# Loading x already transposed and running the 3x3 taps as 32x32 tiles, in a ConvNeXt V2 block

## The chip, the cores and the metric

The kernel runs on one NeuronCore of a Trainium2 chip. The core has a matrix engine (TensorE, PE in the profile; PEld is its loading of weights), three engines for elementwise work (VectorE is DVE, ScalarE is ACT, GpSimd is POOL) and SyncE (SP), which here only issues DMAs. Each engine runs its own instruction stream in order, and semaphores tie the streams together. The metric is device time in microseconds (us) of one execution; lower is better. The kernel before took 1479.03 us, the median of three runs (1475.51 to 1484.01).

## The reference

```
def reference(x, dw, w1, w2, grn_gamma, grn_beta):     # x: (1, 512, 512, 96), bf16
    xp = jnp.pad(x, ((0,0),(1,1),(1,1),(0,0)))
    out = 0
    for i in range(3):
        for j in range(3):
            out = out + xp[:, i:i+H, j:j+W, :] * dw[i, j]          # depthwise 3x3
    h = _layernorm(out, axis=-1)                                  # over the 96 channels
    h = gelu(einsum('bhwc,ce->bhwe', h, w1))                      # 96 -> 384, tanh form
    gx = sqrt((h * h).sum(axis=(1, 2)) + 1e-6)                    # per channel, over the whole image
    nx = gx / (gx.mean(axis=-1) + 1e-6)
    h = grn_gamma * (h * nx) + grn_beta + h
    return x + einsum('bhwe,ec->bhwc', h, w2)                     # 384 -> 96
```

The sum over all pixels in `gx` divides the work in two: nothing of the second product can start before every pixel has gone through the first.

## The kernel before

The image is cut into 128 blocks of 4 rows (2048 pixels). The first phase goes over the blocks in slots, one block a slot for each kind of work, and the kinds are staggered: in slot s the kernel loads x for block s+4, turns block s+3, convolves block s, and runs the first product and the GELU of a block about ten back. A table (`put`, `get`) says what each slot does. Every engine's instructions stay in the order in which the program is written (`InOrder`), so a waiting instruction holds up all that follows it on its engine.

The steps of a block:

- `load_x` (line 216): SP loads the block to `xin`, 128 partitions of 18 neighbouring pixels (16 and one at each side), 3456 bytes on each. Four buffers.
- `turn_x` (line 442): two DVE transposes of 32x32 blocks bring channels onto partitions, into one of five buffers `xT`. Channels 0 to 63 are turned as pairs, so two neighbouring channels lie side by side; `x_rows` (line 450) picks every second column for them.
- `conv_taps` (line 463): 72 matmuls with 64x32 tiles of the matrix engine (64 rows hold two groups of 32 partitions, 32 columns are channels), in three bursts of 24, from `Wq`, a weight tensor built at the start out of `Wd`. The two row halves of one moment write different PSUM banks. The result stands in `Y3`, PSUM banks 4 to 6, or in other banks in a few early slots (`spare`). `burst(0)` ends with a drain of the matrix engine in most slots.
- `evac` (line 496): one ACT instruction copies the three banks to `y_bf`.
- `stage_sq` (POOL, `ysq`), `stage_stats` (24 tiny matmuls that sum `y_bf` and `ysq` over channels), `stage_moments` (DVE), `stage_rstd` and `stage_newton` (POOL, a chain of small operations), `stage_turn` (DVE, `rt`), `stage_rows` (SP, to `r_dram`), `stage_bcast` (SP, four DMAs `rbc` that repeat a row over partitions): these make the layer norm's factor, for a batch of four blocks at a time.
- `stage_norm` (POOL, `yn`), `stage_write` (SP, four DMAs to `yn_dram`), `stage_read` (SP, `ynT`): the normalized block goes through DRAM to come back with 96 channels on partitions.
- `mlp_units` (line 699): the first product in units of one or two PSUM banks, each followed by an ACT instruction that applies GELU into `g`. A quarter of a block is either channel-major (cm: 384 output channels on partitions; DVE's `bn_stats` then gives the sums of squares) or pixel-major (px: the sums of squares come from 12 further matmuls, `gram_next`). `cm_quads` (line 100) says how many of a block's four quarters are cm. Blocks with q % 10 in 0, 3, 7 (`WHOLE`) are kept in DRAM (`g_dram`) with all four quarters cm.

The order written out for one slot with a conv and a first product (lines 886 to 923) is: `conv(0)`, unit(0,2), unit(2,1), squares, `conv(1)`, `turn_x(s+3)`, unit(3,1), unit(4,2), gram, ..., unit(7,1), turn, `conv(2)`, `evac`, gram, unit(8,2), unit(10,1), stats, unit(11,1). On SP the order of a slot is load_x, read, write, bcast, rows, one third of a g store (lines 828 to 838). On POOL it is newton, norm, sq, rstd (lines 839 to 846).

After the last slot the factor `nx` is computed and folded into `W2s`. The second phase then takes the blocks in a fixed order: it recomputes `g` from the normalized blocks, or loads it, or has it still in SBUF; it multiplies by `W2s`, adds x and stores. The change touches nothing that the second phase does, but for the order of columns within a quarter (`quad`, `quad_out`).

Of the kernel before, what the change touches and what calls it, by code (L numbers as in the profile page):

```python
# [9 lines left out]
ACTF = mybir.ActivationFunctionType  # L10
AX = mybir.AxisListType

GR = 4
# [6 lines left out]
WHOLE = (0, 3, 7)  # L20
# [36 lines left out]
def kernel(  # L57
# [11 lines left out]
    f32 = mybir.dt.float32  # L69
    i32 = mybir.dt.int32  # L70
    bf16 = x.dtype
    assert bf16 == mybir.dt.bfloat16

    B, H, W, C = x.shape
# [3 lines left out]
    NI = C // 32  # L78
    NCH = E // 128
    NG = W // 128  # L80
    NBLK = H // GR
    BATCHES = batches_of(NBLK)

    QW = GR * 128
    NQ = GR * W // QW
# [8 lines left out]
    def is_held(q):  # L94
        return q in HELD

    def is_whole(q):
        return q < TAIL0 and q % 10 in WHOLE

    def cm_quads(q):  # L100
        if is_whole(q) or is_held(q):
            return NQ
        if q > HELD[0]:
            return 1
        return 2 if q >= NBLK - 16 or (q - 1) % 10 in WHOLE else 3
# [4 lines left out]
    def chans(i):  # L110
        return slice(i, 64, 2) if i < 2 else slice(64, 96)

    PXP = GR * W // 128
    MB = W // PXP

    def quad(flat_ap, t):
        return flat_ap.rearrange("p r (t g m) -> p t g r m", t=NQ, m=MB)[:, t]

    def quad_out(flat_ap):
        return flat_ap.rearrange("p (g r m) -> p g r m", r=GR, m=MB)  # L120
# [10 lines left out]
    consts = ctx.enter_context(tc.tile_pool(name="consts", bufs=1))  # L131
# [9 lines left out]
    Wq = consts.tile([128, NI, 3, GR, 32], bf16, name="Wq")  # L141
# [12 lines left out]
    parts = consts.tile([128, NCH, NACC + 1], f32, name="parts")  # L154
# [24 lines left out]
    gpool = ctx.enter_context(tc.tile_pool(name="g", bufs=5))  # L179
# [3 lines left out]
    SL = PXP + 2  # L183
    with ExitStack() as p1:
        pe, dve, act, pool, sp = (InOrder(tc, e) for e in (nc.tensor, nc.vector, nc.scalar, nc.gpsimd, nc.sync))
# [3 lines left out]
        def banks(n):  # L189
            if n == 2:  # L190
                return PS[:, 0:2, :]
            ones[0] += 1
            return PS[:, 2 + ones[0] % 2:3 + ones[0] % 2, :]
# [14 lines left out]
        Y3 = PS[:, 4:7, :]  # L208
        pc = p1.enter_context(ExitStack())
        xinpool = pc.enter_context(tc.tile_pool(name="xin", side="right", bufs=4))  # L210
        xins = {}

        def shift(h, j):
            return 1 if (h, j) == (0, GR - 1) else -1 if (h, j) == (1, 0) else 0

        def load_x(b):
            t = xinpool.tile([128, SL, C], bf16, name="xin")
            off = x.offset + b * GR * W * C
            rows = lambda p0, p1, s0, s1: (
                t[p0:p1, s0:s1, :].rearrange("p g c -> p (g c)"),  # L220
                bass.AP(x.tensor, off + (p0 * PXP - 1 + s0) * C, [[PXP * C, p1 - p0], [1, (s1 - s0) * C]]))
            if b == 0:
                pool.memset(t[0:1, 0, :], 0.0)
                parts = [(16, 128, 0, SL), (0, 16, 1, SL), (1, 16, 0, 1)]
            elif b == NBLK - 1:
                pool.memset(t[96:128, SL - 1, :], 0.0)
                parts = [(0, 112, 0, SL), (112, 128, 0, SL - 1), (112, 127, SL - 1, SL)]
            else:
                parts = [(0, 128, 0, SL)]
            for part in parts:  # L230
                o, i_ = rows(*part)
                sp.dma_start(out=o, in_=i_)
            xins[b] = t

        Wd = gpool.tile([128, NQ, NCH, QW], bf16, name="g")[:].rearrange("p t j w -> p (t j w)")[
            :, :NI * 9 * 32].rearrange("p (i k c) -> p i k c", i=NI, k=9)
        zrow = consts.tile([128, W], bf16, name="zrow")
# [4 lines left out]
        for b in range(min(2, NBLK)):  # L242
            load_x(b)
        act.activation(out=warm[:], in_=warm[:], func=ACTF.Gelu_apprx_tanh)
        act.activation(out=Wq[:].rearrange("p i d j c -> p (i d j c)").rearrange("p (a w) -> p a w", a=3),
                       in_=zrow[:, None, :NI * GR * 32].to_broadcast([128, 3, NI * GR * 32]), func=ACTF.Identity)
# [8 lines left out]
        xtpool = pc.enter_context(tc.tile_pool(name="xt", side="right", bufs=1))  # L255
# [6 lines left out]
        NXT = 5  # L262
        xt_ring = []
        xt_all = xtpool.tile([128, NXT, NI, SL * MB], bf16, name="xT")
        for i in range(NXT):
            xt_ring.append(xt_all[:, i])
        assert NXT * NI * SL * MB >= NQ * NCH * QW
        g_over = xt_all[:].rearrange("p x i s -> p (x i s)")[:, :NQ * NCH * QW].rearrange(
# [123 lines left out]
        for i in range(NI):  # L392
            dve.tensor_copy(out=dwx[:, i], in_=dw9[:, None, chans(i)].to_broadcast([9, GR, 32]))
            pe.matmul(Ud[:, i, :], lhsT=dwx[:, i].rearrange("p q c -> p (q c)"), rhs=ident_b[:9, :9],
                      start=True, stop=True)
# [3 lines left out]
        n = 0  # L399
        for h in range(2):  # L400
            for j in range(GR):
                for q in (2 * h, 2 * h + 1):
                    a = q + GR * shift(h, j) - j + 1
                    if 0 <= a < 3:
                        n += 1
                        o, i_ = Wq[32 * q:32 * q + 32, :, :, j, :], Wd[32 * q:32 * q + 32, :, 3 * a:3 * a + 3, :]
                        if n % 2:
                            act.activation(out=o, in_=i_, func=ACTF.Identity)
                        elif n % 4:
                            dve.tensor_copy(out=o, in_=i_)  # L410
                        else:
                            pool.tensor_copy(out=o, in_=i_)

# [28 lines left out]
        def turn_x(b):  # L442
            xin = xins.pop(b)
            t = xt_ring[b % NXT]
            pairs = t[:, 0:2, :].rearrange("p i s -> p (i s)").bitcast(f32)
            dve.transpose(out=pairs.rearrange("p (g m) -> p g m", m=MB),
                          in_=xin[:, :, 0:64].bitcast(f32))
            dve.transpose(out=t[:, 2, :].rearrange("p (g m) -> p g m", m=MB), in_=xin[:, :, 64:96])

        def x_rows(b, p0, p1, i, c0, n):  # L450
            t = xt_ring[b % NXT]
            if i == 2:
                return t[p0:p1, 2, c0:c0 + n]
            return t[p0:p1, 0:2, :].rearrange("p i s -> p (i s)").rearrange(
                "p (s e) -> p s e", e=2)[:, c0:c0 + n, i]

# [6 lines left out]
        def conv_taps(b, spare):  # L463
            if spare:
                Ua, Ub = banks(2), banks(1)
                Y = [Ua[:, 0, :], Ua[:, 1, :], Ub[:, 0, :]]
            else:
                Y = [Y3[:, i, :] for i in range(NI)]
            mms = []
            for n in range(3):  # L470
                mms.append([(h, j, (n + h) % NI, dx) for dx in (0, -1, 1) for j in range(GR) for h in range(2)])
            flat = [m for ms in mms for m in ms]
            first = {}
            last = {}
            for n, (h, j, i, dx) in enumerate(flat):
                first.setdefault((i, j), n)
                last[i, j] = n

            def burst(n, fence=True):
                k = sum(len(ms) for ms in mms[:n])  # L480
                for h, j, i, dx in mms[n]:
                    src = b + shift(h, j)
                    o0, o1 = max(0, -dx), W - max(0, dx)
                    pe.matmul(
                        Y[i][32 * j:32 * j + 32, o0:o1],
                        lhsT=Wq[64 * h:64 * h + 64, i, dx + 1, j, :],
                        rhs=x_rows(src, 64 * h, 64 * h + 64, i, MB * (1 + dx) + o0, o1 - o0)
                        if 0 <= src < NBLK else zrow[64 * h:64 * h + 64, o0:o1],
                        start=first[i, j] == k,
                        stop=last[i, j] == k,  # L490
                    )
                    k += 1
                if n < 2 and fence:
                    pe.drain()

            def evac():
                y = ypool.tile([128, NI, W], bf16, name="y_bf")
                if spare:
                    act.activation(out=y[:, 0:2, :], in_=Ua, func=ACTF.Identity)
                    act.activation(out=y[:, 2, :], in_=Ub[:, 0, :], func=ACTF.Identity)  # L500
                else:
                    act.activation(out=y[:], in_=Y3, func=ACTF.Identity)
                ybf[b] = y

            return [lambda fence=True, n=n: burst(n, fence) for n in range(3)], evac
# [288 lines left out]
        for k, (b0, n) in enumerate(BATCHES):  # L794
# [16 lines left out]
            for b in range(b0, b0 + n):  # L811
# [4 lines left out]
                m = s + (3 if ramp else 4)  # L816
# [4 lines left out]

        busy(FILL[1])
        turn_x(0)
        turn_x(1)
        turn_x(2)
        for s in range(last_slot + 1):
# [34 lines left out]
            elif not mlp:  # L861
                if s + 3 < NBLK:
                    turn_x(s + 3)
# [21 lines left out]
            else:  # L885
                b = mlp[0]
# [9 lines left out]
                if s + 3 < NBLK:  # L896
                    turn_x(s + 3)
# [71 lines left out]
        r = gi[:].bitcast(f32)  # L969
        for it in range(3):  # L970
# [5 lines left out]
            r = rn_[:]  # L976
# [75 lines left out]
```

## Time and profile before

| what | value |
|---|---|
| median of three runs | 1479.03 us (1475.51 to 1484.01) |
| span of the profiled execution | 1480.8 us |
| mean granted TensorE clock | 0.994 |
| first phase, about | 0 to 960 us |
| second phase, about | 960 to 1480 us |
| blocks convolved per slot time, 200 to 490 us | one every 7.03 us |
| from 1100 to 1300 us: DMA share, POOL busy | 1.02, 193.79 of 200 us |

The page's second part is read first: it cuts the span into 40 slices of 37 us.

```profile
PE   8888999999999999999999997789999999999998
...
GB/s 180 179 205 255 241 253 280 228 271 260 260 248 264 258 264 255 276 253 254 263 258 266 263 216 195 195 225 409 366 359 402 417 416 413 419 410 417 411 412 282
```

Up to slice 25 is the first phase, from slice 27 on the second, where the DMA engines move some 410 GB/s. A group's line gives the number of instructions, their busy time together and the mean of one; what follows the bar is the time for which the engine stood idle just before them and what ended it. Busy times overlap: neighbouring instructions of one engine run into each other.

### The profile page before, as it was taken

To read this page: it belongs to the slowest core of one execution; us is meant where nothing else is said; L and a number is where in the kernel's file an instruction comes from. 1 tells how busy PE (TensorE), PEld (TensorE's weight loads), DVE (VectorE), ACT (ScalarE), POOL (GpSimd) and SP (SyncE) were. 2 spreads that over 40 slices of the span, in tenths; PEclk is the share of its full clock that TensorE was granted. 3 is DMA by queue.
4 is the path that set the end of the run, shared out by engine and by line. 5 is a ranking of instruction groups with operands and counts; after the bars stand their busy time and mean duration, and the time that the engine had idled before them with its cause. 6 is when DMAs were issued, how large, how long until landed. Compare 5 with 4: busy or idle time off the path is not lost.

```text
span 1480.8 us, 54225 instructions
## 1 busy us (share of the span) xinstructions
PE 1391.3 (94%) x23125; PEld 810.4 (55%) x23125; DVE 1182.0 (80%) x2135; ACT 1414.4 (96%) x1595; POOL 1300.3 (88%) x922
## 2 busy tenths in 40 slices
PE   8888999999999999999999997789999999999998
PEld 3434444444444444444444445467777777776776
DVE  7849989999999999999999987965555555555555
ACT  7888989999999999999999999999999999999997
POOL 3459889998998999998999987569999999999997
PEclk9999999999999999999999999999999999999999
DMA  5568788788888888888888866669999999999997
GB/s 180 179 205 255 241 253 280 228 271 260 260 248 264 258 264 255 276 253 254 263 258 266 263 216 195 195 225 409 366 359 402 417 416 413 419 410 417 411 412 282
DMA packets 167768, 433.08 MB, mean 292 GB/s; under 512 B 31558, under 2 KB 81318, under 8 KB 163046
## 3 DMA queue, kind: packets, MB, share of 16 engines
q1 hardware_dynamic: 151284, 326.04, 66.3%
q0 software_dynamic: 14880, 103.43, 17.6%
q8 instruction: 181, 2.97, 0.8%
q14 instruction: 61, 0.50, 0.1%
q10 hardware_dynamic: 1362, 0.15, 0.1%
HBM read 273.30 MB, written 156.22 MB: 290 GB/s over the span
## 4 chain that ended last, share of the span: by engine, by line
PE 30%; ACT 24%; DMA 19%; POOL 13%; DVE 6%; issue 4%; SPq 4%; POOLq 0%; ACTq 0%; DVEq 0%
PE PS L35 30%; ACT g L35 16%; DMA out_dram<-o_sb 9%; POOL yn L35 6%; ACT y_bf L35 5%; POOL ysq L35 5%; SPq L35 4%; DMA yn_dram<-yn 3%; DVE bst L35 3%; DMA xin<-in_x_dram 2%; DMA rbc<-r_dram 2%; DMA ynT<-yn_dram 1%; DMA g_dram<-g 1%; DVE o_sb L35 1%; ACT xT L35 1%
## 5 line engine op out<-in xcount | busy, mean ns | idle before, releaser
L35 ACT ACTIVATE g<-PS 128x512 bf16<-128x512 f32 (+2 forms) x1062 | 727.7, 864 | 16.5 <-PE PS L35 15.6
L35 DVE BATCH_NORM_STATS2 bst<-g 128x6 f32<-128x512 bf16 x1110 | 671.3, 672 | 35.4 <-ACT g L35 34.5
L35 PE MATMUL PS<-ynT,w1p 128*128 128x512 bf16 x2181 | 609.6, 381 | 23.6 <-ACT g L35 5.4
L35 ACT ACTIVATE gr<-PS 128x1536 bf16<-128x1536 f32 x360 | 498.5, 1459 | 18.8 <-PE PS L35 13.8
L35 POOL TENSOR_TENSOR yn<-y_bf,rbc 128x1536 bf16<-128x1536 bf16 x126 | 391.3, 3108 | 77.3 <-ACT rbc L35 21.9
L35 DVE TENSOR_TENSOR o_sb<-PS,xb 128x384 bf16<-128x384 f32 x512 | 277.3, 556 | 227.0 <-PE PS L35 190.1
L324 POOL TENSOR_TENSOR xb<-xr,B2c 128x1536 f32<-128x1536 bf16 x118 | 368.1, 3133 | 4.3 <-DVE o_sb L35 2.0
L35 PE MATMUL PS<-xT,Wq 64*32 64x511 bf16 (+1 forms) x9198 | 340.5, 389 | 26.2 <-ACT y_bf L35 8.1
L35 POOL TENSOR_TENSOR ysq<-y_bf 128x1536 bf16<-128x1536 bf16 x114 | 313.6, 2752 | 12.8 <-ACT y_bf L35 12.8
L35 PEld LDWEIGHTS <-w1p 128*128 128x128 bf16 x2181 | 171.6, 98 | 222.0 <-issue 133.4
L35 PEld LDWEIGHTS <-gr 128*128 128x128 bf16 x4296 | 212.1, 98 | 68.9 <-issue 12.0
L35 PE MATMUL PS<-W2s,gr 128*128 128x96 bf16 x4224 | 223.5, 206 | 8.2 <-DVE o_sb L35 8.0
L35 PEld LDWEIGHTS <-Wq 64*32 64x32 bf16 x9216 | 111.9, 90 | 193.3 <-issue 145.9
L35 ACT ACTIVATE y_bf<-PS 128x1536 bf16<-128x1536 f32 (+2 forms) x135 | 199.4, 1482 | 17.4 <-PE PS L35 13.3
L35 DVE STREAM_TRANSPOSE xT<-xin 128x576 f32<-128x576 f32 (+1 forms) x256 | 181.4, 748 | 8.1 <-DMA xin<-in_x_dram 8.1
L35 PEld LDWEIGHTS <-g 128*128 128x128 bf16 x1704 | 104.9, 98 | 86.3 <-issue 54.3
L35 PE MATMUL PS<-w1p,ynT 128*128 128x256 bf16 (+2 forms) x822 | 125.8, 273 | 8.0 <-ACT xT L35 3.2
L35 PE MATMUL PS<-g 128*128 128x128 bf16 x1464 | 122.6, 220 | 2.9 <-DVE PS L35 2.6
L35 PEld LDWEIGHTS <-gl 128*128 128x128 bf16 x1680 | 82.8, 98 | 26.8 <-issue 5.0
L35 PE MATMUL PS<-W2s,gl 128*128 128x96 bf16 x1680 | 89.5, 206 | 3.4 <-DVE o_sb L35 3.2
L35 PEld LDWEIGHTS <-ynT 128*128 128x128 bf16 x822 | 64.1, 97 | 31.5 <-issue 13.7
L279 POOL DMA_DIRECT2D xr<-in_x_dram x115 | 63.7, 555 | 14.2 <-POOL xb L324 14.2
(105 smaller groups left out, 576.5 us busy)
## 6 DMA issues: line engine op xcount, KB each, us to landing
xin<-in_x_dram SPq DMA_DIRECT2D x126, 432.0 KB
g_dram<-g SPq DMA_DIRECT2D x105, 512.0 KB
gl<-g_dram POOLq DMA_DIRECT2D x35, 1536.0 KB, 11.3
yn_dram<-yn SPq DMA_DIRECT2D x512, 96.0 KB
ynT<-yn_dram SPq DMA_DIRECT2D x128, 384.0 KB
out_dram<-o_sb SPq DMA_DIRECT2D x127, 384.0 KB
xr<-in_x_dram POOLq DMA_DIRECT2D x123, 384.0 KB, 6.9
ynT<-yn_dram SPq DMA_DIRECT2D x85, 512.0 KB
```

Source lines behind the costliest of these rows:

```text
L35: r = f(*a, **k)
L279: pq.dma_start(out=xr[:], in_=x[0, r0:r0 + GR].rearrange("r w c -> (r w) c").rearrange("(p g) c -> p g c", g=PXP))
L324: pq.tensor_tensor(out=xb[:], in0=grp[q]["xr"][:], in1=bias[:, None, :].to_broadcast([128, PXP, C]), op=ALU.add)
```

## The change

x is no longer loaded and then turned. One DMA per block reads the block's 512 runs of four pixels (4 x 96 values, 768 bytes) and writes them transposed: the 384 values of a run lie on 128 partitions in three groups k, and the runs lie along the free axis. `xT` is one ring of six blocks. `turn_x`, `x_rows`, `xin` and `Wq` are gone, and the matrix engine reads `Wd` itself.

A value's place now follows from its pixel's phase a (0 to 3 within the run) and channel group i (0 to 2): (k, r) = divmod(3a + i, 4), where r is the quarter of the partitions. A tap in x changes the phase, or at the edge of a run also the column by one; a tap in y shifts the columns by a row of 128. A tap for one phase and channel group is a matmul with a 32x32 tile, from partition quarter r to output quarter a. A block takes 108 such matmuls in three bursts of 36; where the six-block ring wraps (two blocks of six) and at the image's edges a tap in y is cut into two.

The output rows of a block come out ordered by phase, so `evac` reads PSUM with a step of four values and writes `y_bf` in the order that the rest expects, and `quad` and `quad_out` become runs of 128 columns. At last, blocks that follow a whole block have three cm quarters instead of two (34 blocks).

```
-        return 2 if q >= NBLK - 16 or (q - 1) % 10 in WHOLE else 3
+        return 2 if q >= NBLK - 16 else 3
...
-        return slice(i, 64, 2) if i < 2 else slice(64, 96)
+        return slice(32 * i, 32 * i + 32)
...
-        return flat_ap.rearrange("p r (t g m) -> p t g r m", t=NQ, m=MB)[:, t]
+        return flat_ap[:, :, t * 128:(t + 1) * 128]
...
+        NXT = 6
+        xt_all = xtpool.tile([128, NI, NXT * GR, W4], bf16, name="xT")
         def load_x(b):
-            t = xinpool.tile([128, SL, C], bf16, name="xin")
...
+            s0 = b % NXT * GR
+            sp.dma_start_transpose(
+                out=xt_all[:, :, s0:s0 + GR, :].rearrange("p k r w -> p k (r w)"),
+                in_=bass.AP(x.tensor, x.offset + b * GR * W * C, [[4 * C, GR * W4], [1, 4 * C]]))
...
-        def turn_x(b):
-            xin = xins.pop(b)
-            t = xt_ring[b % NXT]
-            pairs = t[:, 0:2, :].rearrange("p i s -> p (i s)").bitcast(f32)
-            dve.transpose(out=pairs.rearrange("p (g m) -> p g m", m=MB),
-                          in_=xin[:, :, 0:64].bitcast(f32))
-            dve.transpose(out=t[:, 2, :].rearrange("p (g m) -> p g m", m=MB), in_=xin[:, :, 64:96])
...
+            src = [(0, 0), (-1, 1), (1, 2)]
+            def rows_of(dy):
+                lo, hi = max(0, -dy), GR - max(0, dy)
+                out = [(lo, hi, b, lo + dy)]
+                if dy and 0 <= b + dy < NBLK:
+                    edge = 0 if dy < 0 else GR - 1
+                    out.append((edge, edge + 1, b + dy, GR - 1 - edge))
+                if len(out) == 2 and abs(out[1][2] % NXT - b % NXT) == 1:
+                    start = b % NXT * GR + dy
+                    return [(0, GR, start)]
+                return [(o0, o1, q % NXT * GR + r0) for o0, o1, q, r0 in out]
             def burst(n, fence=True):
+                dx = src[n][0]
+                for dy in (0, -1, 1):
+                    segs = rows_of(dy)
+                    for o0, o1, r0 in segs:
+                        for L in range(4 * NI):
+                            a, i = divmod(L, NI)
+                            a2 = a + dx
+                            w0, w1_ = (1, W4) if a2 < 0 else (0, W4 - 1) if a2 > 3 else (0, W4)
+                            v0 = w0 - 1 if a2 < 0 else w0 + 1 if a2 > 3 else w0
+                            k, r = divmod(a2 % 4 * NI + i, 4)
+                            pe.matmul(
+                                Y[i][32 * a:32 * a + 32, :].rearrange("p (r w) -> p r w", r=GR)[:, o0:o1, w0:w1_],
+                                lhsT=Wd[32 * r:32 * r + 32, i, 3 * (dy + 1) + dx + 1, :],
+                                rhs=xt_all[32 * r:32 * r + 32, k, r0:r0 + o1 - o0, v0:v0 + w1_ - w0],
...
+            def px_order(ps):
+                return ps.rearrange("p i (q e) -> p i e q", e=NQ)
+            def flat_order(y):
+                return y.rearrange("p i (e q) -> p i e q", e=NQ)
...
-                    act.activation(out=y[:], in_=Y3, func=ACTF.Identity)
+                    act.activation(out=flat_order(y[:]), in_=px_order(Y3), func=ACTF.Identity)
```

The calls of `turn_x` in the slots are gone with it. `load_x(s + 4)` stands where it stood on SP; it now overwrites the place of block s-2, whose last reader is the conv of block s-1, where it used to wait for a free `xin`.

## Prediction

> **What bounds the kernel now.** I read the totals first, then one long steady stretch by engines, then one slot in order of time, then the chain of waits and the DMA queues.
>
> ```profile
> PE 1391.3 (94%) x23125; PEld 810.4 (55%) x23125; DVE 1182.0 (80%) x2135; ACT 1414.4 (96%) x1595; POOL 1300.3 (88%) x922
> ...
> L35 DVE STREAM_TRANSPOSE xT<-xin 128x576 f32<-128x576 f32 (+1 forms) x256 | 181.4, 748 | 8.1 <-DMA xin<-in_x_dram 8.1
> ```
> ```profile
> 204.00:484.00 280.00, 269.00 (x4855) 131.47 (x4852) 278.16 (x477) 280.00 (x399) 258.72 (x188) 1.00 0.83 260
> ```
>
> The second line is the table by stretches (us, then busy time of PE, PEld, DVE, ACT, POOL, clock, DMA share): for 280 us ACT is never idle and DVE idles for 1.8 us. The 181.4 us of DVE transposes are the work to be removed, but an engine beside a full ACT gives nothing back. One slot shows what ACT's fullness consists of:
>
> ```profile
> 507.12 1.61 ACT L35 ACTIVATE y_bf<-PS 128x1536 bf16<-128x1536 f32 x1
> 508.46 5.97 ACT L35 ACTIVATE g<-PS 128x1024 bf16<-128x1024 f32 x9
> 508.79 0.88 PE L35 MATMUL PS<-xT,Wq 64*32 64x512 bf16 x24 [0.15 <-ACT y_bf L35]
> 509.77 0.82 PE L35 MATMUL PS<-ynT,w1p 128*128 128x512 bf16 x3
> ...
> 514.19 1.58 ACT L35 ACTIVATE y_bf<-PS 128x1536 bf16<-128x1536 f32 x1
> ```
>
> Slot: 514.19 - 507.12 = 7.07 us, one y_bf and nine GELUs. In the trace's starts an ACT instruction behind another takes 477 ns for 512 columns, 904 for 1024, 1331 for 1536; a slot's 6, 3 and 1 of them make 2.86 + 2.71 + 1.33 = 6.91 us. The remaining 0.12 to 0.15 us lie at one place: conv(0) may start only when y_bf has left Y3 (508.73), it takes until 509.7 with its drain, and the first GELU of the next block waits behind it. So conv(0), alone among the three bursts, stands on the path.
>
> The other thing on the path is the layer norm's loop:
>
> ```profile
> 491.35 2.75 POOL ysq L35
> ...
> 494.15 1.53 PE PS L35 x31
> ...
> 502.91 2.93 DMA g_dram<-g
> ...
> 506.11 3.11 POOL yn L35
> ```
>
> This is the chain of waits: start, length, what. POOL's yn at 506.11 stood still until a DMA had landed (the rbc just before it), and at 494.15 PE's sums waited for POOL's ysq. Between ysq's end and the matmuls that read it the trace has 5.4 us at 240 us, 3.1 at 293 and 0.1 at 494: every batch of four slots loses 5.3 / 9 = 0.59 us against ACT, and from 494 us on this loop holds ACT up. It runs: yn, ysq, rstd, newton, yn, ysq, yn on POOL (19.2 us), four yn_dram DMAs (2.6), four rbc DMAs (2.7), landing (3.5): 28.0 us against 4 slots of 7.03.
>
> ```profile
> q1 hardware_dynamic: 79947, 154.38, 82.2%
> ```
>
> That is SP's queue from 200 to 800 us: each DMA engine is busy for 0.83 x 7.03 = 5.83 us of a slot.
>
> **The change, part by part**, against the profiled execution of 1480.8 us, which lies 1.8 over the median.
>
> Removed: 256 DVE transposes (-181.4 us) and, with them, a turn in the slot's middle; added: 34 cm quarters, 34 x 3 bn_stats at 671.3 / 1110 = 605 ns, +62 us of DVE. DVE falls to about 1063 us and stays under ACT: 0 on the path. ACT covers it; without it the net 119 us would show. PE loses 34 x 12 matmuls of gram at 56 ns (-23 us), late in the slot, where PE already has 0.2 us of waiting for y_bf to give: 0, at best -20. The build of Wq goes; the first conv starts at 8.08 us, when the warm-up matmuls end: 0. In the ramp two yn wait 0.2 us behind a turn; I take -2 us, bounds 0 and -14 (all ACT idle time from 100 to 200 us and near 893 us, were the loop's stalls to go).
>
> Conv: 9216 matmuls become 15336. In a burst the trace starts eight tiles 3 to 7 ns apart, the next eight 216 ns after the first; twelve tiles make 4 x 6.5 = 26 ns more per burst. For conv(0) in some 105 slots: +3 us. Where the ring wraps (42 blocks) twelve more pairs follow, between 12 x 3 = 40 ns and, by the tiny sum matmuls, 12 x 25 = 300; at 0.1 us: +4. The other two bursts use PE's 0.2 us. Lower bound 0; upper bound, if only eight tiles overlap as now: 36 / 8 x 216 = 0.97 us for 0.65, +0.32 in 105 slots = +34. I take +7, since twelve differs from eight by less than from none.
>
> A rule speaks against this. Before, the tiles that run together write one bank per row half; now a bank is written by four row tiles at once, on different partition quarters. TensorEngine Tiling (Array Packing), Restrictions and Gotchas, says that different row tiles cannot use one PSUM bank at a time. By it a bank's four tiles would follow each other, three in parallel: 36 / 3 x 216 = 2.6 us a burst, and a slot would grow by almost 6 us. No row here shows two row tiles on one bank.
>
> evac reads PSUM with a step of four. No row reads PSUM so. The nearest is the small copy to Wq in pieces, 435 ns for 288 columns where the slope of the plain ones gives 163 + 0.84 x 288 = 405: bounds 0 and +7%, 0.1 us x 128 = +13. I take 0.
>
> The load: SP's issue was 430 ns (median). Bounds 300 ns, the quick rows of rbc, and 2.5 us, the four issues of yn_dram. I take 0.6; in the loop SP has 0.7 us to spare before the yn writes, so it hides; at 2.5 us some 1.4 stick out in 25 batches, +35. The load also has a new wait, for conv(s-1). Behind it on SP stand ynT, the yn writes and rbc; POOL waits for rbc, PE for ynT two slots on. At 277.39 and 284.65 us the load went out 3 us before that conv ended, but the yn writes then waited for POOL anyway; in the slot with rbc it was 0.7 us (266.14 against 266.85). That eats slack once: +2.
>
> The transfer itself: 8 packets of 3456 bytes per engine, 135 ns each (median), were 1.08 us. The new one reads 256-byte pieces, 96 per engine. Packets of 64 bytes take 11 ns and of 1024 bytes 46, so 18 for 256: 1.73 us, +0.65 per load. Bounds: the old rate per byte, 0.96 us (-0.12); and pieces of 32 bytes (16 rows of two bytes on a partition), 768 x 10 = 7.7 us (+6.6). I take 256-byte pieces, the nearer kind to what is read. The load stands in the rings before rbc, so the loop grows by about 0.6 us: 1.2 lost per batch instead of 0.59, the slack of 5.4 us at 240 us is gone after 4.5 batches, and 18 batches lose 1.2 where 14 lost 0.59: 22 - 8 = +14.
>
> DMA: Bandwidth & Descriptors, Latency and other measured facts, gives a transposing DMA 261 GB/s where rows are not contiguous. By it a load would be 1.5 us, and the +14 would shrink to about +8.
>
> Sum: 1480.8 - 2 + 7 + 2 + 14 = 1502 in the profiled execution, **1500** against the median.
>
> **Rivals.**
> Faster: the load costs an engine no more than before (-0.12 us), each block arrives three slots early instead of one, DVE answers the turn at once, and the loop's stalls (about 14 us of ACT idle time) go: 1479 - 14 = 1465. For it: DVE waited 8.1 us for xin, and rt came 4 us after newton. Against: ACT's floor of 6.91 us a slot stands. It decides as soon as a load takes under 1.3 us of each engine.
> No change: every term within 7 us of nothing: 1479.
> DMA becomes the bound: from 7.03 - 5.83 + 1.38 = 2.6 us per load on (1.38 is the old one's mean). At 4 us a slot lasts 8.45, and 118 of them give +168: about 1647; at the far bound, 7.7 us, 2083. For it: a DMA share of 0.83 leaves little. Against: fewer bytes than before.
> SP becomes the bound: its issues fill 0.72 of a slot; at 2.5 us per load it is full, 1535 as worked out above.
> That the tiles do not overlap gives 1479 + 34 = 1513, within the forecast's range.
>
> **How the numbers follow.** Forecast 0.42, faster 0.24, no change 0.14, DMA-bound 0.13, SP-bound 0.07. A measurement of this kernel tells 0.5% (7.4 us) from no change. Faster by more: 0.24 + 0.02 of the forecast's low side = 0.26; same: 0.14; slower: 0.60. The likeliest case alone spans 1487 to 1530 (the terms at 0 and the conv at its upper bound). The range goes down to 1460, the faster case with 5 us to spare, and up to 1580, a load of 3.4 us; that leaves out some 0.08 above and 0.07 below.
>
> **What would show it.** Right: DVE near 1063 us and idle in every slot, ACT above 98% from 204 to 484 us, slots of 7.05 to 7.15, conv bursts of 24 ns more, POOL's yn waiting for rbc in more batches and before 400 us, a DMA share of 0.87 to 0.92. Wrong: a DMA share at 1.0 with PE and ACT idle in the first phase; bursts over 1 us; issues of xT on SP over 1.5 us; y_bf above 1.45 us where it stands alone; or a first phase shorter than 950 us, which would say that the loop and not ACT set it.

## The result, and the profile after

The changed kernel takes 1542.33 us, the median of four runs (1538.77 to 1547.03), where the kernel before takes 1480.74 beside it: a ratio of 1.041, with a 95% interval from 1.0377 to 1.0444. It is slower by 62 us (56 to 66); 1500 was forecast. The profiled execution spans 1540.4 us, 59.6 more than that of before, and the explanation is made against these 59.6.

First, where in the span they lie. The trace gives every start of `y_bf`, one for a block (two for the seven blocks in other banks). The 28th start marks the end of the ramp, the last one the end of the convolutions:

| us | ramp, to the 28th y_bf | steady, 28th to last (106 blocks) | rest | span |
|---|---|---|---|---|
| before | 132.2 | 751.5 | 597.1 | 1480.8 |
| changed | 141.4 | 802.6 | 596.4 | 1540.4 |

So 9 us go in the ramp, 51 in the steady stretch, and nothing after it. The engines' totals and the table by stretches of the changed kernel, in the columns shown for the kernel before:

```profile
PE 1402.1 (91%) x28735; PEld 852.5 (55%) x28735; DVE 1088.7 (71%) x1982; ACT 1416.7 (92%) x1588; POOL 1296.1 (84%) x917
```
```profile
204.00:484.00 280.00, 253.63 (x6185) 134.75 (x6165) 237.18 (x407) 263.69 (x374) 244.47 (x186) 0.98 1.04 237
```

DVE is relieved of its transposes, ACT has as much to do as before (1416.7 against 1414.4). But in the 280 us in which ACT was never idle it now stands still for 16.3, no engine is full, and the DMA share has gone from 0.83 to 1.04 while fewer bytes move (237 against 260 GB/s). That share suggests that the DMA engines are the bound; the experiments will show that SP's issues are the larger part. One slot, in the timeline (start, length, engine, instructions, idle time before them):

```profile
499.59 1.58 ACT L35 ACTIVATE y_bf<-PS 128x1536 bf16<-128x1536 f32 x1
501.22 0.86 PE L35 MATMUL PS<-xT,Wd 32*32 32x512 bf16 x36 [0.16 <-ACT y_bf L35]
506.57 1.63 ACT L35 ACTIVATE y_bf<-PS 128x1536 bf16<-128x1536 f32 x1
```

An undisturbed slot still lasts 506.57 - 499.59 = 6.98 us, and a burst of 36 takes no longer than a burst of 24 did (0.86 against 0.88). The loss is in some slots only, about one in four. Such a one, with SP's queue and POOL in order of time:

```profile
439.92 2.10 SPq L35 DMA_DIRECT2D yn_dram<-yn  x2
442.06 2.08 SPq L35 DMA_DIRECT2D rbc<-r_dram  x4
444.24 1.85 SPq L35 DMA_TRANSPOSE xT<-in_x_dram  x1
446.20 0.51 SPq L35 DMA_DIRECT2D ynT<-yn_dram  x1
446.77 2.50 SPq L35 DMA_DIRECT2D yn_dram<-yn  x4
447.94 3.10 POOL L35 TENSOR_TENSOR yn<-y_bf,rbc 128x1536 bf16<-128x1536 bf16 x1 [3.55 <-DMA rbc<-r_dram]
...
450.00 2.50 SPq L35 DMA_TRANSPOSE xT<-in_x_dram  x1
...
461.25 2.75 POOL L35 TENSOR_TENSOR ysq<-y_bf 128x1536 bf16<-128x1536 bf16 x1
464.06 0.45 PE L35 MATMUL PS<-rowsel,ysq 128*128 128x4 bf16 x12 [3.19 <-POOL ysq L35]
464.79 0.60 ACT L35 ACTIVATE g<-PS 128x512 bf16<-128x512 f32 x1 [1.86 <-PE PS L35]
```

Read it downwards. From 439.92 to 449 SP hardly rests: one issue follows the other within 0.1 us. The four `rbc` come out at 442.06, when SP has got to them; POOL has waited 3.55 us when they have landed, its `ysq` ends 3 us late two slots on, PE's sums wait 3.19 us for it, and the GELUs 1.86 for the matmuls queued behind those sums. Summed up from 200 to 900 us (waiting instruction, what ended the wait, us, times, longest):

```profile
PE PS L35 <- POOL ysq L35: 29.6, 18, 3.3
PE PS L35 <- ACT y_bf L35: 14.3, 45, 0.6
PE PS L35 <- issue: 6.0, 10, 1.3
```

The first was 6.2 us before:

```profile
PE PS L35 <- POOL ysq L35: 6.2, 4, 2.8
```

And SP's issues of the load (ns shortest/median/longest, first and last start), before and after, say why SP is late:

```profile
L35 SPq DMA_DIRECT2D xin<-in_x_dram x85: 343/430/1993, 200.9 to 799.6; - x85
```
```profile
L35 SPq DMA_TRANSPOSE xT<-in_x_dram x80: 1327/2113/2947, 202.1 to 799.8; - x80
```

A transposing load holds SP for 2.1 us where the plain one took 0.43 (medians).

A wait of PE does not end with itself. At the end of what is shown above, the table by stretches (columns as before) reads:

```profile
462.40:465.80 3.40, 1.58 (x62) 1.05 (x63) 3.22 (x6) 1.12 (x3) 3.40 (x2) 1.00 0.67 142
465.80:469.20 3.40, 3.40 (x53) 1.20 (x54) 1.36 (x3) 1.59 (x3) 3.40 (x2) 0.50 0.85 224
```

PE had been busy for 1.58 of 3.4 us, and for the next 3.4 us it was granted half its clock (0.50): it is full there, and ACT still starves. The steady stretch of the changed kernel holds 41 us at half clock (6.8 before), and 25 of the 54 us for which ACT stands idle in it fall there. In the steady stretches of all kernels of this document PE was busy for at most 0.76 of the 3.4 us before each such time. So the lower clock follows the waits and adds to them; no run holds the clock fixed, so the order in time is all that shows this.

### The profile page after: what moved, and what is told of

It reads as the page before. It is cut to its first block, busy times and chain, and to the rows that moved or that the text cites. A ratio compares the mean times of both kernels' runs of the same rounds, so it can differ in the third digit from the quotient of the medians.

```text
span 1540.4 us, 65191 instructions
## 1 busy us (share of the span) xinstructions
PE 1402.1 (91%) x28735; PEld 852.5 (55%) x28735; DVE 1088.7 (71%) x1982; ACT 1416.7 (92%) x1588; POOL 1296.1 (84%) x917
## 5 line engine op out<-in xcount | busy, mean ns | idle before, releaser
L35 DVE BATCH_NORM_STATS2 bst<-g 128x6 f32<-128x512 bf16 x1212 | 734.5, 676 | 111.3 <-ACT g L35 110.6
L35 PE MATMUL PS<-ynT,w1p 128*128 128x512 bf16 x2283 | 650.3, 384 | 31.6 <-ACT g L35 8.6
L35 PE MATMUL PS<-xT,Wd 32*32 32x512 bf16 (+2 forms) x15336 | 360.4, 369 | 43.2 <-ACT y_bf L35 20.9
L35 PEld LDWEIGHTS <-Wd 32*32 32x32 bf16 x15336 | 181.5, 90 | 253.4 <-issue 202.1
L35 PEld LDWEIGHTS <-w1p 128*128 128x128 bf16 x2283 | 182.5, 98 | 199.5 <-issue 115.7
L35 ACT ACTIVATE y_bf<-PS 128x1536 bf16<-128x1536 f32 (+2 forms) x135 | 196.5, 1461 | 34.6 <-PE PS L35 34.0
L35 PE MATMUL PS<-w1p,ynT 128*128 128x384 bf16 (+2 forms) x618 | 97.5, 273 | 7.6 <-ACT xT L35 3.2
L35 PEld LDWEIGHTS <-g 128*128 128x128 bf16 x1296 | 79.6, 98 | 44.6 <-issue 19.7
L35 PE MATMUL PS<-g 128*128 128x128 bf16 x1056 | 88.8, 221 | 1.3 <-DVE PS L35 1.3
L35 PE MATMUL PS<-rowsel,ysq 128*128 128x4 bf16 x1536 | 57.0, 166 | 34.6 <-POOL ysq L35 33.6
L35 PEld LDWEIGHTS <-ysq 128*128 128x128 bf16 x1536 | 47.5, 96 | 36.7 <-POOL ysq L35 35.7
```

Of the source, the lines that this page charges most:

```text
L35: r = f(*a, **k)
```

## The experiments

The theories: **A**, the load's 256-byte pieces fill the DMA engines; **B**, its long issue fills SP; **C**, the load waits on SP for a conv, and the layer norm's DMAs stand behind it; **D**, the conv's longer bursts, above all where the ring wraps. The table has all runs. SP is the sum of its issues from 200 to 800 us for one block, in brackets the load's part; "ysq" and "instr" are PE's waits from 200 to 900 us for POOL's `ysq` and for its own instructions ("issue" in the profile).

| kernel | SP us a block | DMA share | ysq | instr | ramp | steady | ratio to before (95%) |
|---|---|---|---|---|---|---|---|
| before | 4.91 (0.57) | 0.83 | 6.2 | 0 | 132.2 | 751.5 | 1 |
| changed | 6.60 (2.13) | 1.04 | 29.6 | 6.0 | 141.4 | 802.6 | 1.041 (1.038-1.044) |
| plain | 5.23 (0.70) | 0.84 | 6.0 | 6.6 | 141.5 | 762.3 | 1.009 (1.006-1.012) |
| plain256 | 6.93 (2.29) | 0.85 | 51.3 | 0.6 | 144.9 | 822.6 | 1.057 (1.053-1.061) |
| plain5 | 7.94 (3.47) | 0.70 | 102.5 | 0.3 | 154.7 | 938.7 | 1.140 (1.136-1.145) |
| late | 6.53 (2.14) | 1.02 | 37.6 | 4.4 | 148.8 | 800.9 | 1.045 (1.040-1.050) |
| ring8 | 6.68 (2.17) | 1.02 | 34.6 | 6.6 | 139.1 | 807.7 | 1.039 (1.037-1.042) |
| quads | 6.58 (2.14) | 1.01 | 32.1 | 7.1 | 144.6 | 811.1 | 1.044 (1.042-1.047) |
| before_sp | 6.54 (2.26) | 0.84 | 25.1 | 0 | 134.4 | 782.4 | 1.020 (1.016-1.024) |
| nowrap | 6.53 (2.16) | 1.03 | 34.8 | 0 | 140.3 | 799.4 | 1.035 (1.030-1.040) |
| plain_nowrap | 5.22 (0.69) | 0.84 | 9.9 | 4.4 | 134.3 | 758.7 | 1.005 (1.002-1.008) |
| yn1_after | 4.02 (1.59) | 0.97 | 0 | 38.7 | 142.3 | 798.4 | 1.052 (1.048-1.057) |
| yn1_plain | 3.00 (0.57) | 0.75 | 0 | 47.9 | 141.5 | 812.7 | 1.048 (1.043-1.053) |
| yn1_plain256 | 4.59 (2.10) | 0.87 | 0.2 | 15.5 | 144.3 | 766.7 | 1.037 (1.030-1.043) |
| yn1_nowrap | 4.44 (1.79) | 1.04 | 0 | 21.6 | 134.5 | 769.2 | 1.029 (1.024-1.034) |
| yn1_ring8 | 5.11 (2.39) | 1.03 | 0 | 46.6 | 149.5 | 813.2 | 1.056 (1.052-1.061) |
| yn4_after | 5.91 (2.05) | 1.08 | 10.1 | 15.0 | 146.0 | 781.1 | 1.041 (1.038-1.045) |
| yn4_plain | 4.34 (0.63) | 0.83 | 0 | 12.1 | 138.8 | 762.6 | 1.022 (1.019-1.025) |
| yn1_before | 2.76 (0.61) | 0.80 | 0 | 0 | 131.2 | 746.1 | 0.999 (0.997-1.001) |
| yn1b_before | 2.79 (0.68) | 0.80 | 0 | 0 | 131.3 | 746.1 | 1.007 (1.004-1.010) |

### The load without its transposition: plain, plain256, plain5

```
# plain: one issue, 1024-byte pieces
-            sp.dma_start_transpose(out=xt_all[:, :, s0:s0 + GR, :]..., in_=...)
+            sp.dma_start(out=xt_all[:, :, s0:s0 + GR, :].rearrange("p k r w -> p k (r w)"),
+                in_=bass.AP(x.tensor, x.offset + b * GR * W * C, [[NI * W, 128], [W, NI], [1, W]]))
# plain256: for k in range(NI), one issue each, 256-byte pieces
+                sp.dma_start(out=xt_all[:, k, s0:s0 + GR, :],
+                    in_=bass.AP(..., [[NI * W, 128], [NI * W4, GR], [1, W4]]))
# plain5: as plain, on partitions 0-15, 16-31, 32-63, 64-95, 96-127
```

> The transposing load is replaced by a plain load of the same 393 KB into the same ring slot, in one issue and in pieces of 1024 bytes; the transposition of x is left out. Conv, ring, waits and the order on SP stay as in the changed kernel. Theory A (the 256-byte pieces of the transposing load fill the DMA engines, about 3.0 us of each engine per load instead of 1.35): falls from 1542 to about 1490, DMA share in 200-800 us back from 1.03 to about 0.85. Theory B (SP is the bound because an issue takes it 2.1 us instead of 0.43): also about 1490, so the two need the next runs. Theory C (the load now waits on SP for a conv, with the layer norm's DMAs queued behind it): stays at 1530 to 1545. Theory D (more and longer conv bursts, PE short of instructions where the ring wraps): stays at 1530 to 1545.

> As the plain load, but in 256-byte pieces on both sides (three issues, one per channel block; the transposition is left out): the number and size of the pieces is that of the transposing load. Theory A: pieces of 256 bytes cost the engines the same without a transposition, so 1530 to 1545 with a DMA share near 1.0; if instead the crossbar is what makes a piece slow (32 ns mean, 18 median), the share is about 0.9 and the time 1490 to 1505. Theory B: three issues of about 0.45 us are 1.4 us of SP, 1500 to 1515. Theories C and D: 1530 to 1545.

> As the plain load in 1024-byte pieces, but in five issues over parts of the partitions, so that SP is busy for about 2.1 us per load as with the transposing one, and the DMA engines are not (the transposition is left out). Theory A: as the plain load, within 8 us. Theory B: 1530 to 1545. Theories C and D: no difference to the plain load.

Plain: 1499.22 us (1495.37 to 1504.95), so the transposing load is worth 1.041 - 1.009 = 0.032 of 1481, some 47 us, and the rest of the change 13. C and D, as the load's explanation, fall with it, as the plain load has the same wait and the same conv. Plain256: 1570.29 (1566.81 to 1575.41), slower than the changed kernel though its DMA engines are hardly busier than those of before. Plain5: 1693.56 (1691.58 to 1698.79), from the bytes and pieces of plain in five issues instead of one; its DMA engines are the idlest of all. I had expected 1530 to 1545 there, since I took an issue for 0.43 us; it was 0.69 in the mean. In the table, from changed down to nowrap, the steady stretch and the wait for `ysq` follow SP's column and not that of the DMA share; only before_sp, which has the old conv and load, lies 18 us under late at the same sum. In the slow kernels the slot is SP's sum and 0.8 to 1.0 us more (changed, plain256 and plain5, 600 us by the blocks in them: 7.59, 7.69 and 8.82 us against 6.60, 6.93 and 7.94), as if SP set their pace; before_sp, below, tests that alone. The half clock takes its part: it covers 41, 68 and 205 us of their steady stretches, and 3.4 in plain.

### The load's wait and the other parts: late, ring8, quads

```
# late: load_x(s + 4) moved behind store_next()
# ring8
-        NXT = 6
+        NXT = 8
# quads
-        return 2 if q >= NBLK - 16 else 3
+        return 2 if q >= NBLK - 16 or (q - 1) % 10 in WHOLE else 3
```

> The changed kernel with one edit: in a slot the load of x is issued on SP after the layer norm's DMAs (read, write, broadcast, rows, store) instead of before them. Theory C: the DMAs behind the load no longer wait for the conv nor for its 2.1 us issue, so about 1500. Theory B: SP's total work is the same, 1530 to 1545. Theory A: the rings are as full, but the small DMAs of the loop stand before the load in them and not behind: 1520 to 1540. Theory D: 1540.

> The changed kernel with a ring of eight blocks of xT instead of six: the load no longer waits for the conv of the slot before but for one two slots earlier, long done; SP can run ahead. Theory C: 1490 to 1510 and SP's waits for PE fall from 226 us to under 60. Theory B: SP's sum is the same, 1530 to 1545. Theory A: 1530 to 1545. Blocks that wrap fall from two in six to two in eight: theory D gives a quarter of its share back, 1525 to 1535.

> The changed kernel with the channel-major quarters of before (two instead of three in the blocks that follow a whole one): 34 x 3 bn_stats fewer on DVE, 34 x 12 gram matmuls more on PE. All theories of the load: within 8 us of 1542. If DVE's added 62 us were what costs: 1500 to 1520.

Late gave 1549.59 us (1549.01 to 1560.98), ring8 1544.56 (1539.94 to 1546.80), quads 1551.71 (1547.57 to 1554.41): none is faster than the changed kernel. C falls: in another place in the order, or without the wait, SP has the same sum to do. In ring8 SP's waits for PE were 200.6 us (226.3 in the changed kernel) and not under 60 as expected, so most of them were never the load's. The 62 us of added `bn_stats` cost nothing.

### SP's load put on the kernel before: before_sp

```
-                parts = [(0, 128, 0, SL)]
+                parts = [(p, p + 32, 0, SL) for p in range(0, 128, 32)]
```

> The kernel before with one edit: its plain load of x in four issues of 32 partitions instead of one, the same bytes in the same 3456-byte pieces, nothing left out. SP's time for a load goes from 0.57 to some 2.0 us, near the 2.13 of the transposing issue; conv, ring, waits and DMA packets stay as before. Theory B (SP full is the steady loss of the changed kernel): 1510 to 1535, PE waits for POOL's ysq of 20 to 40 us. Theory A (the DMA engines): 1479 to 1487.

1517.34 us (1513.74 to 1520.57), within B's 1510 to 1535 and far from A's 1479 to 1487. Nothing but the number of issues differs from the kernel before: its group of loads on SP, its stretch and its wait for `ysq`, in the columns from above:

```profile
L35 SPq DMA_DIRECT2D xin<-in_x_dram x324: 310/427/2066, 199.0 to 797.9; - x162
```
```profile
200.00:800.00 600.00, 561.31 (x9940) 269.80 (x9924) 571.66 (x972) 572.78 (x811) 535.98 (x406) 0.97 0.84 248
```
```profile
PE PS L35 <- POOL ysq L35: 25.1, 16, 3.2
```

With 2.26 us of SP for a load the kernel before has the same late `ysq` (25.1 us against 29.6 in the changed kernel), at a DMA share of 0.84. That is B shown by itself: 0.020 of 1481, 30 us, of the 47 that the transposing load costs. The other 17 appear only together with the new conv and load; I did not separate them, and a share of the fuller DMA engines in them (theory A) is not excluded.

### SP relieved in the changed kernel: yn1_after, yn1_plain, yn1_plain256

`yn_dram` is kept phase by phase, so that `yn` goes out in one issue; it is read back in pieces of 1024 bytes.

```
-        return yn_dram[q].rearrange("c (r w) -> c r w", r=GR)
+        return bass.AP(yn_dram[q].tensor, yn_dram[q].offset, [[W, C], [C * W, GR], [1, W]])
...
-            for r in range(GR):
-                sp.dma_start(out=yn_dst(b, r), in_=yn[32 * r:32 * r + 32, :, :])
+            sp.dma_start(out=yn_dst(b), in_=yn[:].rearrange("p i w -> p (i w)"))
```

> The changed kernel with the layer norm's write to yn_dram in one SP issue instead of four (yn_dram is kept phase by phase, so that the write is whole rows of 3072 bytes and the read of ynT is 4 pieces of 1024 bytes a row): nothing is left out. The transposing load, its 256-byte pieces and its wait stay; SP's work per block falls by some 1.9 us of about 6.7. Theory B (SP is the bound): 1495 to 1515. Theory A (the DMA engines are full, share 1.03): 1530 to 1545. Theory C (the load's wait for a conv holds up what is behind it): 1515 to 1535, since there is less behind it.

> The changed kernel with both: one issue for the write of yn, and the plain load in 1024-byte pieces (the transposition of x is left out). Two limits side by side (SP full; and, once SP has room, DMA engines so full that PE's instructions come late): with both gone 1480 to 1492, ACT idle 200-800 us under 8 us (37 with one issue alone, 10 with the plain load alone), PE's waits for instructions under 10 us (38.7). If the longer conv (D) held a share by itself: PE's waits for instructions stay above 25 us and the time above 1505.

> The same with the plain load in 256-byte pieces (three issues; the transposition is left out): as many and as small pieces as the transposing load, 18 ns each where that one's take 32 in the mean. If it is the crossbar's slow pieces that fill the engines: 1482 to 1500 and PE's waits for instructions under 12 us. If small pieces as such: 1535 to 1560 and above 25 us. If SP is still the limit (three issues instead of one): PE waits for POOL's ysq come back, 1505 to 1530.

Yn1_after: 1559.73 us (1557.58 to 1570.31), slower, where B promised 1495 to 1515. What B says did happen: SP fell to 4.02 us a block, and PE's waits for `ysq` from 29.6 us to nothing. But another wait took their place:

```profile
518.80 0.78 PE L35 MATMUL PS<-xT,Wd 32*32 32x512 bf16 x29
521.46 0.41 PE L35 MATMUL PS<-xT,Wd 32*32 32x384 bf16 x19 [1.88 <-issue]
522.04 1.45 ACT L35 ACTIVATE y_bf<-PS 128x1536 bf16<-128x1536 f32 x1 [1.72 <-PE PS L35]
```

This is one burst of a wrapped block, cut in the middle. "Issue" means that PE waited for no semaphore: after 29 of the 48 matmuls it had no instructions for 1.88 us, and ACT stood still for 1.72. The DMA queue marked "instruction" moved 225 blocks of 16384 bytes; PE's 28735 matmuls and as many weight loads make 64 bytes each, and 181 blocks in the kernel before also come to 64 for each of its 46250. So PE's instructions come by DMA, 256 at a time. PE's position settles that these blocks are what it waits for: from 200 to 900 us the changed kernel and its variants have 247 "issue" waits of 0.2 us or more before a matmul, all at the same place in the count modulo 256 (within one instruction), and all end 1.2 to 1.8 us after a block has landed. If a block is called due when PE starts on the 256 instructions before such a place, I estimate from these starts (200 to 800 us) that it begins 1.5 us after that in the kernel before, 2.0 in the changed one and 2.7 in yn1_after, takes 1.1 us, and that PE has by then used up 92, 142 and 180 of its 256 in the mean; PE ran dry only where it had used over some 160.

Yn1_plain, 1556.82 (1549.53 to 1569.57) where I expected 1480 to 1492, decides against A a second time: with neither SP nor the DMA engines full (0.75) it is as slow as yn1_after, with no wait for `ysq` and 47.9 us of waits for instructions. In yn1_plain256, 1540.08 (1524.08 to 1546.22), where SP takes 1.6 us longer over a block, they are 15.5 us. Of these three, the kernel whose SP has least to do has most of them.

### Why instructions come late: yn1_ring8, yn4_after, yn4_plain

```
# yn4: the layout of yn1, written in four issues of 32 partitions
+            for r in range(GR):
+                sp.dma_start(out=yn_dst(b)[32 * r:32 * r + 32], in_=yn[32 * r:32 * r + 32]...)
```

> The changed kernel with one issue for the write of yn and a ring of eight blocks. With the single write SP waited 501 us for the conv that its load overwrites and then issued a slot's DMAs in one go; with eight blocks it needn't wait for it. If that bunching is why PE's instructions come late (2.5 us after they are due, 1.8 in the changed kernel): waits of PE for instructions fall from 38.7 to under 20 us, POOL's for rbc from 54 to under 25, time 1515 to 1540. If not: 1545 to 1560.

> The changed kernel with yn_dram kept phase by phase as in the single-write kernel, the same 3072- and 1024-byte pieces, but written in four issues of 32 partitions as before; nothing is left out. If it was SP's quick issuing that made PE's instructions late there: PE's waits for instructions go back to about 6 us (38.7 there) and the waits for POOL's ysq come back to about 30 us, as SP is full again; 1550 to 1560 with the second phase's 17 us for smaller pieces. If the layout or its pieces make them late: 30 us or more of waits for instructions.

> The same with the plain load of x (the transposition is left out): it differs from the kernel with single write and plain load (1557) only in the number of issues for the write of yn. If quick issuing makes instructions late: PE's waits for them fall from 48 to under 12 us, and 1508 to 1520, though SP has more to do. If the layout does: 1545 to 1560.

Yn1_ring8 was a miss: 1571.96 us (1565.46 to 1575.41), waits for instructions 46.6 us. Taking away the load's wait does not bring the instructions sooner. Yn4_plain, 1516.35 (1515.85 to 1521.34), is by ratio (1.022 against 1.048) 38 us faster than yn1_plain, from which it differs in the number of issues alone. PE's waits in yn1_plain, then in yn4_plain:

```profile
PE PS L35 <- issue: 47.9, 44, 3.4
```
```profile
PE PS L35 <- issue: 12.1, 16, 1.8
```

So one issue in place of four makes PE wait longer for its instructions. That it does so because SP's slow issuing had spread the transfers, and that the instruction blocks stand behind other transfers in the DMA engines, is my reading: it fits their later start (by the same estimate 2.8 us after they are due against 1.9), but no record shows the place where they wait. Yn4_after took 1545.12 (1540.58 to 1547.48), a little under the 1550 to 1560 expected, and its waits for instructions lie between the two expectations (6 and 30): an issue of whole rows is shorter, so SP is relieved by 0.7 us, the wait for `ysq` falls to 10.1 us, that for instructions rises to 15.0, and the steady stretch is 21 us shorter than in the changed kernel, at the highest DMA share of all (1.08). The changed kernels with this layout lose 14 to 19 us in the rest of the span (611 to 615 us against 596.4), where `yn_dram` is now read in 1024-byte pieces.

### The wrapped bursts: nowrap, yn1_nowrap, plain_nowrap

```
-                return [(o0, o1, q % NXT * GR + r0) for o0, o1, q, r0 in out]
+                return [(o0, o1, q % NXT * GR + r0) for o0, o1, q, r0 in out[:1]]
```

> The changed kernel without the second segment of a conv burst where the ring wraps (the taps over the edge row at the ring's seam are left out in 42 blocks), and nothing else. If the wrapped bursts cost in the ramp and SP in the steady stretch: the ramp (28th y_bf, 141.4 us) comes back to about 134, the steady stretch stays near 800 us: 1530 to 1537. If the wraps cost in the steady stretch too, as with the single yn write: 1505 to 1520.

> The changed kernel with one issue for the write of yn, and without the second segment of a conv burst where the ring wraps (the taps over the edge row at the ring's seam are left out in 42 blocks): PE has 3024 instructions fewer and no burst of 96 instructions. If the wrapped bursts run PE out of instructions: its waits for them fall from 38.7 us to under 15 and the time from 1560 to 1530 to 1540. If instructions come late everywhere because the DMA engines are full: 30 us or more stay, 1552 to 1560.

> The plain load (1024-byte pieces, one issue, no transposition) and no wrapped bursts (edge taps at the seam left out): what is left against the kernel before is the longer bursts of 36 and the load's wait. By the plain load alone 1499; the ramp's 9 us and some of the steady 11 should go: 1482 to 1490. If the longer bursts as such cost: 1494 to 1499.

Yn1_nowrap took 1526.95 us (1518.03 to 1532.67): without bursts of 48 the ramp is back at 134.5 us and the steady stretch falls by 29, so much of what PE lacked was in them; 21.6 us of waits for instructions remain, where under 15 were expected. Plain_nowrap took 1494.74 (1484.35 to 1499.98), above the 1482 to 1490 expected and in the range named for longer bursts as such; in its profile the ramp is 134.3 us against 141.5 in plain. By ratio the wraps cost 1.009 - 1.005, about 6 us, and the rest of the conv and the load's place 7; the two intervals overlap, so the first of these is not firm. Nowrap took 1538.92 (1533.84 to 1541.83): with SP full the steady stretch stays (799.4), as expected, but the ramp did not come back (140.3), which I cannot explain.

### The single write in the kernel before: yn1_before, yn1b_before

Yn1_before is the single write of `yn` in the kernel before; yn1b_before also reads 96 rows instead of 128 in the second phase.

```
+        return bass.AP(yn_dram[q].tensor, yn_dram[q].offset, [[W, C], [C * W, GR], [1, W]])
...
-                    sq.dma_start(out=ynt[:], in_=yn_rows(q))
+                    sq.dma_start(out=ynt[:C], in_=yn_rows(q))
```

> The kernel before with the same single issue for the write of yn. If the layer norm's loop is what costs the kernel before its 0.59 us per batch, a loop shorter by about 1.9 us ends that: 1465 to 1475. If ACT's own time sets it: 1476 to 1482.

> The kernel before with one issue for the write of yn, and with the second phase's read of it limited to the 96 rows that count (393 instead of 524 KB, as it now comes in pieces of 1024 bytes). Nothing is left out. The first phase was without ACT idle time with the single issue (0.1 us in 200-800 us instead of 3.9), and the second lost 12 us to the smaller pieces: if the shorter read gives those back, 1468 to 1475; if not, 1480 to 1485.

1483.78 us (1479.06 to 1486.88), no difference, and 1495.38 (1489.32 to 1505.26), slower by 0.7%. In the steady stretch the single write gains 5 us, and ACT is idle for 0.1 us of 600 there (4.2 before); the rest of the span takes 606.2 us, and with 96 rows 616.8, instead of 597.1. The shorter read, meant to give that back, made it worse. No version here is faster than the kernel before.

## Why the prediction was right or wrong

The direction was right, and 1542 lies in the range of 1460 to 1580, but by luck: the forecast case had a third of the loss, and its mechanism, a longer transfer that delays `rbc`, is not the one that the runs showed. What happened is the rival that had a chance of 0.07, "SP becomes the bound", at 1535.

**The step that failed** is the issue of the load: "Bounds 300 ns, the quick rows of rbc, and 2.5 us, the four issues of yn_dram. I take 0.6; in the loop SP has 0.7 us to spare before the yn writes, so it hides". It measured 2.1 us, and nothing hid it: about the same issue time alone, put on the kernel before, cost 30 us. The far bound was priced about right, though for a narrow reason: 1.4 us in 25 batches, +35, counts only the slot with `rbc`, where the runs show that SP's whole sum, with 0.8 to 1.0 us around it, has to fit in the slot: 4.91 - 0.57 + 2.13 = 6.47, and 0.9, is 7.37 against the 7.06 that a block took before (600 us by 85). The price also left out that PE's waits are followed by half clock. The likelihood was wrong because I looked for the nearest row by size and not by kind: no row of the trace of before shows a transposing issue, and then both bounds had deserved weight.

**The transfer**, +14 us as it delays `rbc`: the loop was late, but in the slot shown because SP came late to the issue of `rbc`. The median piece took 18 ns, as forecast; the mean was 32, so 96 pieces are 3.1 us of each engine and not 1.73 (nor the 1.5 of the other estimate), and the DMA share was 1.04 instead of 0.87 to 0.92. What the longer transfer itself cost is not separated; it can be in the 17 us left open above. The share was my sign for "DMA becomes the bound", and it misled: plain256 is slower at 0.85, yn4_after has a shorter steady stretch at 1.08.

**The wait for conv(s-1)**, +2: ring8 shows nothing of it. That agrees.

**Conv**, +3 for the bursts and +4 for the wraps: the runs give about 7 (with all else that stays with the plain load) and 6. Together 13 where 7 were forecast, with the 6 not firm, and the mechanism of the second was another: I priced the added matmuls at 0.1 us a block; the trace shows them as a longer ramp and as PE without instructions, which the list of resources did not have.

**The rule against the tiles**: the Trainium skill, TensorEngine Tiling (Array Packing), Restrictions and Gotchas, says that different row tiles cannot use one PSUM bank at a time. The changed kernel has four row tiles on one bank, and its bursts of 36 take 0.86 us, not 2.6. Here the measurement decides against the page, for tiles on different partition quarters.

**Removed work**: DVE went down to 1088.7 us, forecast 1063, and no run shows that it was worth anything, as said: quads, with 62 us less of `bn_stats` on DVE, is no faster. The ramp, -2 forecast, was +9. **evac**, 0: `y_bf` alone lasts 1.45 us with the step of four as without; right.

**Signs named in advance**: issues of xT over 1.5 us on SP was named as one that would show the forecast wrong, and it was the one that counted. A DMA share of 1.0 with PE and ACT idle came too, and pointed the wrong way. ACT above 98% from 204 to 484 us was wrong (94%), and so were bursts 24 ns longer (0.86 us against 0.88); POOL's `yn` waiting for `rbc` before 400 us was right.

## What to carry to other kernels

Sum up the instructions of a queue-issuing engine for one slot, gaps included, like those of any other engine, and compare with the slot before changing the kind or number of its DMAs: here four plain issues in place of one, with nothing else altered, cost the kernel before 30 us. A DMA share of 1.0 is a reason to test the DMA engines, not a finding; the test is to change pieces and issues separately. When one limit is lifted, look for the wait that takes its place before counting the gain: a second one may lie just behind it.

## What the runs showed of the hardware

- A transposing issue of 393 KB holds SP for 2.1 us in the changed kernel (median), where it mostly follows another issue within 0.3 us, and for 1.4 in yn1_after, where it never does; yn1_nowrap has both, 2.5 and 1.5. A plain one of the same bytes takes 0.59 (plain). Why the issue before it matters is open.
- 256-byte pieces took 18 ns in the mean as plain DMA and 32 when transposed (medians 18 in both).
- PE's instructions arrive by DMA in blocks of 256, and PE can wait for them: up to 47.9 us of 700 (yn1_plain). The Trainium skill, Runtime: NRT & Kernel Launch, Instruction fetch mechanics, states the blocks of 256 and that the fetch is mostly hidden. The blocks agree with the trace (64 bytes an instruction); hidden it is in the kernel before (no such wait), and not in yn1_plain or yn1_after, where short matmuls come in bursts of up to 48 and SP writes `yn` in one issue.
- Fewer, larger issues on SP made a kernel slower (yn1_plain 1557 us, yn4_plain 1516), with 47.9 us of waits for those instructions instead of 12.1.
- The granted clock of PE fell to 0.50, mostly for 3.4 us at a time, after 3.4 us in which PE was busy for at most 0.76: 41 us of the changed kernel's steady stretch, 205 of plain5's, 6.8 before.
